# Other row and part orders for the spectrum and z transfers of an FFT convolution followed by a soft mixture of experts

## The chip, the cores and the metric

The kernel runs on one core of one Trainium2 chip. The metric is device time in microseconds of one execution, lower is better. The time before is 910.25 us, the median of 3 runs (909.78 to 915.08). All data are 4-byte floats.

## The reference

A long convolution of 8 sequences (5696 positions, 128 channels) with one filter through the FFT, and behind it a soft mixture of experts with 32 slots over all 45568 positions:

```python
Xf = np.fft.rfft(x, n=L, axis=1)              # x: (8, 5696, 128), L = 2*5696
Hf = np.fft.rfft(h, n=L, axis=0)
y = np.fft.irfft(Xf * Hf[None], n=L, axis=1)[:, :S, :]
x = y.reshape(B * S, D)
logits = x @ phi                              # (45568, 32)
d = softmax(logits, axis=0)                   # over the positions
slot_input = (d.T @ x).reshape(8, 4, 128)
slot_out[e] = np.maximum(slot_input[e] @ w1[e], 0) @ w2[e]
c = softmax(logits, axis=1)                   # over the slots
return c @ slot_out
```

## The kernel before

The transform is done as matrix products in two steps, with N1 = 90 and N2 = 64. A position is n1 * 64 + n2, and a frequency has a first index k (90 values) and a second one. The 64 values of n2 are used in two halves of 32: HALF = 32, and the columns n2 and 63 - n2 are added and subtracted beforehand, on GpSimd (`fold`, L217). A chunk is CH = 4 columns n2 of one half; a group is one sequence, or the filter (group 0), and has NJ = 8 chunks, so there are 9 x 8 = 72 chunks.

**Stage A** (`stage_a`) transforms one chunk along n1. For the frequencies below LOW (here 60) it makes 2 x 2 matmuls with 64 columns of the table s1 into two PSUM banks; ScalarE copies them to a tile fst of 128 rows x 4 KB (L243), in which rows 0 to 63 belong to one half and rows 64 to 127 to the other. For the frequencies from LOW on ("high") it does this once for two chunks, in four strips of 32 rows. The tile goes to the spectrum buffer f in DRAM, laid out as frequency, n2, real and imaginary, channel. One DMA is issued for each half (60 rows x 4 KB), and for a high tile one for each chunk and half (30 rows x 4 KB). The tile has 4 buffers.

**Stage B** (`load_g`, `stage_b1`, `stage_b2`) takes 8 frequencies at a time: it loads gt (128 rows: frequency parity and n2; 4 frequencies of 1 KB each), multiplies with the table wt (L284), multiplies with the filter's spectrum on VectorE (L304, L312), multiplies with the table vt (L327), and copies the result z to the tile zst (L332). In zst the rows alternate between two parts o = 0, 1. The first MAIN = 64 frequencies go to the buffer zm in DRAM (part, frequency, n2 half index r, real and imaginary, channel), one DMA for each part with every second row; the other 26 go to the buffer zr in four DMAs (or with shorter rows).

**Stage C** takes 8 values of r at a time, a "pair" T; there are 32 pairs. `load_main` loads zc from zm (128 rows: part and frequency; 8 KB each), `load_rest` loads zx from zr. `stage_c1` multiplies with the tables im and ir (L412, L417), and the rest of stage C does the soft mixture's logits and sums. There is one zc buffer in the main loop; after it, a second one called zd is added.

The order is written out by hand. A step t of the main loop does stage A of chunk t, stage B of up to two units of an earlier group (`slot_b`, LAG_B = 9 steps behind), and in every second step stage C1 of the pair T = (t - 27)/2. Stage A's and B's stores are put into a list `pending`, and `flush()` issues them (all carry the line L225). Nearly all DMAs are issued by SP's queue, in order: a DMA whose buffer or data isn't ready holds up those behind it. The issues there: x loads (L198), f, zm and zr stores (L225), gt loads (L270, three ahead), zc loads (L374, issued after the C1 of the pair before), zx loads (L385).

After the loop come the last pairs, the experts' products, and the output: 24 stores of 768 or 1024 KB (L897) and one last store of 256 KB (L901), which writes the last 64 positions of all 8 sequences:

```python
out=ov[:, NV * RW * N2:, :].rearrange("b (j n) d -> b j (n d)", n=CH),
in_=o_[:, n, :, :].rearrange("p q d -> p (q d)"))
```

Its DRAM side is 8 batches x 16 rows x 2 KB, its SBUF side 128 rows x 2 KB.

Of the kernel before, what the change touches and what calls it, by code (L numbers as in the profile page):

```python
# [11 lines left out]
F32 = mybir.dt.float32  # L12
# [6 lines left out]
def transform_tables(S, N1, N2, CH, LOW, MAIN, XR):  # L19

    N, R1, HALF, P = N1 * N2, S // N2, N2 // 2, 2 * N2
    k1 = np.arange(N1)  # L30
    alpha = np.pi * (k1 + 0.5) / N1
    m1 = np.arange(R1) - (N1 - 1) / 2
    a1 = np.outer(m1, alpha)
    part = np.stack([np.cos(a1), -np.sin(a1), -np.cos(a1)], 1)
    s1 = np.zeros((P, 2, 3, N2 + HALF))
    for i, r in enumerate((slice(0, R1), slice(XR - R1, XR))):
        s1[r, i, :, 0:LOW] = part[:, :, 0:LOW]
        s1[r, i, :, N2:N2 + N1 - LOW] = part[:, :, LOW:]
    a0 = np.outer(alpha, np.arange(N1 // 2) + 0.5)
    part = np.stack([np.cos(a0), -np.sin(a0), -np.cos(a0)], 1)  # L40
    NP = N1 // 2
    im = np.zeros((2, MAIN, 2, N2))
    ir = np.zeros((2, 2, HALF, N2))
    for o in range(2):
        for c in range(2):
            im[o, :, c, 0:NP] = part[0:MAIN, o + c]
            ir[o, c, 0:N1 - MAIN, 0:NP] = part[MAIN:, o + c]
    k2 = np.arange(N2)
    omega = np.pi * (k1[:, None] + 2 * N1 * k2[None] + 0.5) / N
    m2 = np.arange(HALF) - (N2 - 1) / 2  # L50
    a2 = m2[None, :, None] * omega[:, None, :]
    w = np.concatenate([np.cos(a2), np.sin(a2)], 1)
    back = np.arange(N2).reshape(2, HALF).T.reshape(-1)
    NU = (NP + 1) // 2
    turn = (N1 - 1) / 2 * alpha[:, None] + (N2 - 1) / 2 * omega
    wq = np.zeros((2, N2, NP, N2))
    vq = np.zeros((2, N2, NU, 2, N2))
    tn = np.zeros((2, N2, 2, (NU + 1) // 2, 2, 2))
    for a in range(2):
        wq[a] = w[a::2].transpose(1, 0, 2)  # L60
        for q in range(NP):
            vq[q % 2, :, q // 2, a] = w[2 * q + a][back].T
            tn[q % 2, :, 0, q // 4, a, q // 2 % 2] = np.cos(turn[2 * q + a]) / N
            tn[q % 2, :, 1, q // 4, a, q // 2 % 2] = np.sin(turn[2 * q + a]) / N
    im, ir, wq, vq, tn = [t.reshape(P, *t.shape[k:]) for t, k in
                          ((im, 2), (ir, 3), (wq, 2), (vq, 2), (tn, 2))]
    return [np.ascontiguousarray(t, dtype=np.float32) for t in (s1, im, ir, wq, vq, tn)]
# [3 lines left out]
def kernel(  # L71
# [24 lines left out]
    nc = tc.nc  # L96
    P = 128
    B, S, D = x.shape
    NSL = moe_phi.shape[1]
    E, _, F = moe_w1.shape  # L100
    SPE = NSL // E
    NFC = F // P
    N1, N2 = 90, 64
    R1, HALF, NP = S // N2, N2 // 2, N1 // 2
    CH = 4
    NJ = HALF // CH
# [5 lines left out]
    HP = P // 2  # L112
    NQ = NJ // 2
    assert S == R1 * N2 and R1 == N1 - 1 and D == P and CH == Q == 4
    LOW, MAIN = 60, HP
    XR = -(-R1 // 16) * 16
    ctx.enter_context(tc.manual_schedule())

# [1 line left out]
        nc.inline_tensor(t, f"tab_{n}").ap()  # L120
        for n, t in zip(("s1", "im", "ir", "w", "v", "turn"),
                        transform_tables(S, N1, N2, CH, LOW, MAIN, XR))]
    fd = [nc.dram_tensor(f"f_{g}", (N1, N2, 2, D), F32, kind="Internal").ap() for g in range(B + 1)]
    zm = [nc.dram_tensor(f"zm_{b}", (2, MAIN, HALF, 2, D), F32, kind="Internal").ap() for b in range(B)]
    zr = [nc.dram_tensor(f"zr_{b}", (2, 2, HALF, HALF, D), F32, kind="Internal").ap() for b in range(2)]
    cd = nc.dram_tensor("c_t", (P, B * NQ, Q, 2, MH), F32, kind="Internal").ap()

# [23 lines left out]
    front = ExitStack()  # L151
# [69 lines left out]
    pending = []  # L221
# [8 lines left out]
    def stage_a(c, high):  # L230

        g, j = divmod(c, NJ)
        st = apool.tile([P, CH, 2, D], F32, name="fst", tag="fst", bufs=4)
        if high:
            groups = [(c_, o, HALF, slice(HP, HP + HALF)) for c_ in (c - 1, c) for o in range(2)]
        else:
            groups = [(c, o, HP, slice(0, HP)) for o in range(2)]
        for q in range(2):
            p = bank()
            for i, (c_, o, m, cols) in enumerate(groups):  # L240
                nc.tensor.matmul(p[i * m:(i + 1) * m, :], s1[:, g // B, q + o, cols], columns(c_, o),  # L241
                                 start=True, stop=True)
            nc.scalar.activation(st[:, :, q, :],  # L243
                                 p[:, :].rearrange("p (n d) -> p n d", d=D), AF.Copy)
        k0, k1 = (LOW, N1) if high else (0, LOW)
        for i, (c_, o, m, _) in enumerate(groups):
            n0 = o * HALF + CH * (c_ % NJ)
            pending.append(partial(
                nc.sync.dma_start,
                out=fd[g][k0:k1, n0:n0 + CH, :, :].rearrange("k n c d -> k (n c d)"),  # L250
                in_=st[i * m:i * m + k1 - k0, :, :, :].rearrange("k n c d -> k (n c d)")))
        if high:
            for c_ in (c - 1, c):
                del folded[c_]
# [61 lines left out]
    def stage_b2(u):  # L316
        g, w, us = parts(u)
        if g == 0:
            return
        m = len(us)  # L320
        y_ = prods.pop(u)
        bz = bps.tile([P, 2, 2, 2 * D], F32, name="bz", tag="bz")
        for o, (i, n) in enumerate(us):
            for q in range(n):
                r = slice(q * HP, (q + 1) * HP)
                for a in range(2):
                    nc.tensor.matmul(bz[a * HP:(a + 1) * HP, q, o, :], vt[r, i, a, :],  # L327
                                     y_[r, a * m + o, :, :].rearrange("p c d -> p (c d)"),
                                     start=True, stop=True)
        n = us[0][1]  # L330
        st = bpool.tile([P, 2, 2, 2 * D], F32, name="zst", tag="zst", bufs=3)
        nc.scalar.activation(st[:, 0:m, 0:n, :].rearrange("p o q x -> p q o x"),  # L332
                             bz[:, 0:n, 0:m, :], AF.Copy)
        k = m * n
        sv = st[:, :, :, :].rearrange("p o q x -> p (o q) x")
        for o in range(2):
            if 8 * w < MAIN:
                pending.append(partial(
                    nc.sync.dma_start,
                    out=zm[g - 1][o, 8 * w:8 * w + 2 * k].rearrange("(q a) r c d -> (a r) q (c d)", a=2),  # L340
                    in_=sv[o::2, 0:k, :]))
                continue
            k0 = 8 * w - MAIN
            for c in range(2):
                pending.append(partial(
                    nc.sync.dma_start,
                    out=zr[g % 2][o, c, k0:k0 + 2 * k].rearrange("(q a) r d -> (a r) q d", a=2),
                    in_=sv[o::2, 0:k, c * D:(c + 1) * D]))
# [17 lines left out]
    def load_main(T):  # L366
        if T >= NT:
            return
        b, j = divmod(T, NQ)
        t_ = zring.pop(0)  # L370
        zring.append(t_)
        zs[T] = t_
        n = 2 * CH
        nc.sync.dma_start(  # L374
            out=t_[0][:, :, :, :, :].rearrange("p h n c d -> p (h n c d)"),
            in_=zm[b].rearrange("o k r c d -> (o k) r (c d)")[:, j * n:(j + 1) * n].rearrange(
                "p r x -> p (r x)"))

    def load_rest(T):
        if T >= NT:  # L380
# [243 lines left out]
    for i in range(8):  # L624
        nc.scalar.dma_start(
            out=zr[i // 4][i // 2 % 2, i % 2, N1 - MAIN:].rearrange("k (j r) d -> (k j) (r d)", r=2 * CH),
            in_=zring[0][1][0:4 * (HALF - N1 + MAIN), :, :, :].rearrange("p h n d -> p (h n d)"))
# [114 lines left out]
    for q in range(Q):  # L742
        r = slice(q * NSL, (q + 1) * NSL)
        nc.gpsimd.tensor_copy(out=rep4[r, :, :],
                              in_=ident[r, r].unsqueeze(1).broadcast_to([NSL, Q, NSL]))
# [17 lines left out]
    for V in range(T, NT):  # L763
# [30 lines left out]
        else:  # L794
            for i in range(4 * (V - T - 1), min(4 * (V - T), E), 2):
                nc.sync.dma_start(
                    out=w2s[:, i:i + 2, :, :],
                    in_=moe_w2[i:i + 2].rearrange("e (p c) d -> p e c d", p=P))
# [6 lines left out]
    p = bank()  # L805
# [8 lines left out]
    p = bank()  # L814
# [5 lines left out]
                  ap=[own.ap[0], [NSL + SPE, E], [1, SPE]])  # L820
# [6 lines left out]
    for g in range(EG):  # L827
        for f0 in range(0, F, FH):
            p = bank()
# [3 lines left out]
            dst = hid[:, g, :, f0 // NFC:(f0 + FH) // NFC]  # L833
# [6 lines left out]
    for g in range(EG):  # L840
        for k0 in range(0, NFC, 4):
            p = bank()
            for k in range(4):
# [3 lines left out]
                out=hidT[:, g, k0:k0 + 4, :], in_=p[:, :].rearrange("p (k c) -> p k c", k=4))  # L847
# [9 lines left out]
    p = bank()  # L857
# [18 lines left out]
    for b in range(B):  # L876
        for w0 in range(0, NV, G4):
            n = min(G4, NV - w0)
# [10 lines left out]
            for q in range(Q):  # L889
                dst = o_[:, 0:n + lone, q, :]  # L890
# [7 lines left out]
                out=ov[b, t0:t0 + n * RW * N2, :].rearrange("(w p n) d -> p w (n d)", p=P, n=CH),  # L898
                in_=o_[:, 0:n, :, :].rearrange("p w q d -> p w (q d)"))
            if lone:  # L900
                nc.sync.dma_start(  # L901
                    out=ov[:, NV * RW * N2:, :].rearrange("b (j n) d -> b j (n d)", n=CH),
                    in_=o_[:, n, :, :].rearrange("p q d -> p (q d)"))
# [29 lines left out]
```

## Time and profile before

| | |
|---|---|
| median of 3 runs | 910.25 us |
| the profiled execution, its time | 909.23 us |
| its span, first to last instruction | 907.4 us |
| PE (TensorE matmul) busy | 760.2 us, 84% |
| PEld (weight load) busy | 387.7 us, 43% |
| DVE (VectorE) busy | 601.4 us, 66% |
| ACT (ScalarE) busy | 436.8 us, 48% |
| POOL (GpSimd) busy | 399.8 us, 44% |
| mean granted TensorE clock | 0.903 |
| DMA, all queues | 278.33 MB, 307 GB/s |
| HBM read / written | 147.94 / 129.00 MB |
| ACT waiting at L243 for an f store (free fst) | 27.6 us in 11 waits |
| PE waiting at L284 for a gt load | 33.0 us in 10 waits |
| first and last f store issued | 15.2 and 656.2 us |
| first and last zc load issued | 175.7 and 767.3 us |

The span is the profiled execution's, and the work is counted within it. The page gives the busy time of each engine, the span in 40 slices with a digit for tenths of busy time, the DMA queues, and the chain of waits that ended last, followed back from the end. The DMA share is the mean of the 16 DMA engines' busy share; overlapping packets can take it above 1. In a list of groups, `f<-fst` reads "f written from fst".

### The profile page before, as it was taken

To read this page: it belongs to the slowest core of one execution; us is meant where nothing else is said; L and a number is where in the kernel's file an instruction comes from. 1 tells how busy PE (TensorE), PEld (TensorE's weight loads), DVE (VectorE), ACT (ScalarE), POOL (GpSimd) and SP (SyncE) were. 2 spreads that over 40 slices of the span, in tenths; PEclk is the share of its full clock that TensorE was granted. 3 is DMA by queue.
4 is the path that set the end of the run, shared out by engine and by line. 5 is a ranking of instruction groups with operands and counts; after the bars stand their busy time and mean duration, and the time that the engine had idled before them with its cause. 6 is when DMAs were issued, how large, how long until landed. Compare 5 with 4: busy or idle time off the path is not lost.

```text
span 907.4 us, 21291 instructions
## 1 busy us (share of the span) xinstructions
PE 760.2 (84%) x8308; PEld 387.7 (43%) x8308; DVE 601.4 (66%) x896; ACT 436.8 (48%) x880; POOL 399.8 (44%) x353
## 2 busy tenths in 40 slices
PE   6857778689999989999998999799888877767893
PEld 2212233234444444444444444344444434344793
DVE  2029767568778867886877787678778766653552
ACT  2423234335556545665655655456544444563441
POOL 4634322444555655655655566456332224651000
PEclk9979889999999999999999999899988888766855
DMA  8989999999999999999999999999998768540798
GB/s 267 318 275 343 293 296 337 298 314 376 341 291 375 361 326 308 372 358 299 357 364 335 295 373 348 303 308 346 306 291 304 264 200 341 186 166 1 292 406 335
DMA packets 170443, 278.33 MB, mean 307 GB/s; under 512 B 13543, under 2 KB 128231, under 8 KB 165135
## 3 DMA queue, kind: packets, MB, share of 16 engines
q1 hardware_dynamic: 169336, 275.74, 89.7%
q10 hardware_dynamic: 1008, 1.25, 0.5%
q8 instruction: 66, 1.08, 0.5%
q14 instruction: 33, 0.27, 0.1%
HBM read 147.94 MB, written 129.00 MB: 305 GB/s over the span
## 4 chain that ended last, share of the span: by engine, by line
PE 47%; DMA 23%; ACT 8%; POOL 8%; DVE 6%; issue 6%; SPq 1%; ACTq 0%; DVEq 0%; POOLq 0%
PE bank L241 9%; DMA gt<-f 9%; PE bt L284 9%; PE bz L327 6%; POOL y L430 5%; PE bank L412 4%; DMA f<-fst 4%; PE op L886 3%; PE bank L439 3%; PE bank L417 3%; PE bank L448 2%; DMA zx<-zr 2%; ACT fst L243 2%; DMA out_dram<-o 2%; PE bank L527 2%
## 5 line engine op out<-in xcount | busy, mean ns | idle before, releaser
L241 PE MATMUL bank<-x,s 128*32 128x512 f32 (+1 forms) x1152 | 218.0, 620 | 12.9 <-POOL x L217 8.4
L217 POOL TENSOR_TENSOR x<-xc 128x512 f32<-128x512 f32 x144 | 180.4, 1278 | 107.2 <-PE bank L241 86.5
L284 PE MATMUL bt<-gt,wt 64*64 64x256 f32 x1620 | 125.0, 419 | 72.8 <-DMA gt<-f 33.0
L430 POOL TENSOR_TENSOR y<-y,op 128x512 f32<-128x512 f32 x64 | 77.6, 1213 | 206.8 <-DVE op L404 204.3
L304 DVE TENSOR_TENSOR pi<-bt,Hi 128x1024 f32<-128x1024 f32 x96 | 113.0, 1177 | 83.5 <-PE bt L284 83.3
L243 ACT ACTIVATE fst<-bank 128x512 f32<-128x512 f32 x216 | 122.8, 592 | 86.0 <-PE bank L241 57.7
L332 ACT ACTIVATE zst<-bz 128x1024 f32<-128x1024 f32 x96 | 93.3, 972 | 128.3 <-PE bz L327 109.4
L284 PEld LDWEIGHTS bt<-gt,wt 64*64 64x64 f32 x1620 | 58.3, 141 | 151.2 <-issue 79.1
L312 DVE TENSOR_TENSOR yf<-bt,pi 128x512 f32<-128x512 f32 x192 | 119.4, 663 | 3.3
L304 DVE TENSOR_TENSOR bt<-bt,Hr 128x1024 f32<-128x1024 f32 x96 | 113.0, 1177 | 0.0
L241 PEld LDWEIGHTS bank<-x,s 128*32 128x32 f32 (+1 forms) x1152 | 55.1, 126 | 129.8 <-issue 93.6
L327 PE MATMUL bz<-yf,vt 64*64 64x256 f32 x1440 | 110.4, 404 | 0.0
L327 PEld LDWEIGHTS bz<-yf,vt 64*64 64x64 f32 x1440 | 64.3, 143 | 25.5 <-issue 4.2
L512 POOL TENSOR_TENSOR L<-L,rs 128x512 f32<-128x512 f32 x32 | 33.5, 1048 | 91.6 <-DVE rs L511 66.4
L404 DVE TENSOR_TENSOR y<-bank,y 128x512 f32<-128x512 f32 x32 | 22.1, 692 | 76.7 <-ACT y L420 76.5
L439 PE MATMUL bank<-ident,y 109*128 109x109 f32 x512 | 62.7, 273 | 7.9 <-ACT yt L441 7.9
L504 ACT ACTIVATE L<-L 128x512 f32<-128x512 f32 x32 | 20.2, 630 | 94.7 <-POOL L L501 94.6
L430 POOL TENSOR_TENSOR y<-y,om 128x512 f32<-128x512 f32 x54 | 63.9, 1183 | 2.1
L439 PEld LDWEIGHTS bank<-ident,y 109*128 109x128 f32 x512 | 52.9, 149 | 19.4 <-POOL x L217 14.7
L412 PE MATMUL bank<-zc,im 64*64 64x512 f32 x480 | 60.8, 623 | 0.0
L441 ACT ACTIVATE yt<-bank 128x360 f32<-128x360 f32 x128 | 53.0, 482 | 7.7 <-PE bank L439 7.3
L420 ACT ACTIVATE y<-bank 128x512 f32<-128x512 f32 x32 | 19.1, 596 | 72.6 <-PE bank L417 72.6
(101 smaller groups left out, 862.5 us busy)
## 6 DMA issues: line engine op xcount, KB each, us to landing
gt<-f SPq DMA_DIRECT2D x99, 512.0 KB
f<-fst SPq DMA_DIRECT2D x144, 240.0 KB
zm<-zst SPq DMA_DIRECT2D x128, 256.0 KB
zc<-zm SPq DMA_DIRECT2D x30, 1024.0 KB
xc<-in_x_dram SPq DMA_DIRECT2D x32, 768.0 KB
f<-fst SPq DMA_DIRECT2D x144, 120.0 KB
out_dram<-o SPq DMA_DIRECT2D x16, 1024.0 KB
zx<-zr SPq DMA_DIRECT2D x30, 512.0 KB
```

Of the source, the lines that this page charges most:

```text
L217: nc.gpsimd.tensor_tensor(out=y_[:, o, :, :], in0=near, in1=far, op=AL.subtract if o else AL.add)
L241: nc.tensor.matmul(p[i * m:(i + 1) * m, :], s1[:, g // B, q + o, cols], columns(c_, o), start=True, stop=True)
L243: nc.scalar.activation(st[:, :, q, :], p[:, :].rearrange("p (n d) -> p n d", d=D), AF.Copy)
L284: nc.tensor.matmul(bt[q * HP:(q + 1) * HP, a, o, :], wt[r, 2 * i + q, :], t_[r, 2 * o + q, :, :].rearrange("p c d -> p (c d)"), start=True ...
L304: nc.vector.tensor_tensor(out=p_, in0=pv, in1=h_, op=AL.mult)
L312: nc.vector.tensor_tensor(out=y_[r, 0:k, c, :], in0=pv[:, :, c, :], in1=pi[r, 0:k, 1 - c, :], op=op_)
L327: nc.tensor.matmul(bz[a * HP:(a + 1) * HP, q, o, :], vt[r, i, a, :], y_[r, a * m + o, :, :].rearrange("p c d -> p (c d)"), start=True, sto ...
L332: nc.scalar.activation(st[:, 0:m, 0:n, :].rearrange("p o q x -> p q o x"), bz[:, 0:n, 0:m, :], AF.Copy)
L412: nc.tensor.matmul(ps[o, c][h_ * HP:(h_ + 1) * HP, :], im[r, c, :], zt[r, h_, :, c, :], start=True, stop=False)
L430: eng.tensor_tensor(out=part_, in0=part(v, 0), in1=o_[:, :, :], op=sign)
L439: nc.tensor.transpose(p[:, i * TR:(i + 1) * TR], ys[T][0:TR, k * CH + i, 0:D], ident[0:TR, 0:TR])
L441: nc.scalar.activation(yt[:, k * CH:(k + 1) * CH, :, :], of_tokens(p), AF.Copy)
```

## The change

The frequencies are split at 64 in place of 60 (LOW = HP = 64). The low tile then has 64 + 64 full rows, and the high tile 4 strips of 32 rows of which 26 hold frequencies and 6 are empty (zero columns of s1). f gets 64 + 32 = 96 rows of frequencies, so that the empty ones have a place. Each fst tile is stored by one DMA of 128 rows, whose DRAM side is written out as a pattern with three dims. In f the n2 then stand in the order chunk, half, column in place of half, chunk, column, and the table wt's rows are permuted (`front`) to match.

z's rows for the first 64 frequencies come out of the product with vt by part and then r (no `back` permutation for them), and zm is laid out as frequency, part, r. A unit's z goes out in one DMA of 128 rows in place of two of 64. The zc load then reads zm through a pattern of part, frequency, row.

```diff
+    front = np.arange(N2).reshape(2, HALF // CH, CH).transpose(1, 0, 2).reshape(-1)
...
-        wq[a] = w[a::2].transpose(1, 0, 2)
+        wq[a] = w[a::2].transpose(1, 0, 2)[front]
         for q in range(NP):
-            vq[q % 2, :, q // 2, a] = w[2 * q + a][back].T
+            vq[q % 2, :, q // 2, a] = w[2 * q + a][back if 2 * q >= MAIN else slice(None)].T
...
-    LOW, MAIN = 60, HP
+    LOW, MAIN = HP, HP
...
-    fd = [nc.dram_tensor(f"f_{g}", (N1, N2, 2, D), F32, kind="Internal").ap() for g in range(B + 1)]
-    zm = [nc.dram_tensor(f"zm_{b}", (2, MAIN, HALF, 2, D), F32, kind="Internal").ap() for b in range(B)]
+    fd = [nc.dram_tensor(f"f_{g}", (LOW + HALF, N2, 2, D), F32, kind="Internal").ap() for g in range(B + 1)]
+    zm = [nc.dram_tensor(f"zm_{b}", (MAIN, 2, HALF, 2, D), F32, kind="Internal").ap() for b in range(B)]
...
-        k0, k1 = (LOW, N1) if high else (0, LOW)
-        for i, (c_, o, m, _) in enumerate(groups):
-            n0 = o * HALF + CH * (c_ % NJ)
-            pending.append(partial(
-                nc.sync.dma_start,
-                out=fd[g][k0:k1, n0:n0 + CH, :, :].rearrange("k n c d -> k (n c d)"),
-                in_=st[i * m:i * m + k1 - k0, :, :, :].rearrange("k n c d -> k (n c d)")))
+        k0, m = (LOW, HALF) if high else (0, LOW)
+        j0 = j - high
+        v = fd[g][k0, 2 * CH * j0]
+        dst = [[CH * 2 * D, P // m], [N2 * 2 * D, m], [1, CH * 2 * D]]
+        pending.append(partial(
+            nc.sync.dma_start,
+            out=bass.AP(tensor=v.tensor, offset=v.offset, ap=dst),
+            in_=st[:, :, :, :].rearrange("p n c d -> p (n c d)")))
...
+        if 8 * w < MAIN:
+            pending.append(partial(
+                nc.sync.dma_start,
+                out=zm[g - 1][8 * w:8 * w + 2 * k].rearrange("(q a) o r c d -> (a o r) q (c d)", a=2),
+                in_=sv[:, 0:k, :]))
+            return
         for o in range(2):
-            if 8 * w < MAIN:
-                pending.append(partial(
-                    nc.sync.dma_start,
-                    out=zm[g - 1][o, 8 * w:8 * w + 2 * k].rearrange("(q a) r c d -> (a r) q (c d)", a=2),
-                    in_=sv[o::2, 0:k, :]))
-                continue
...
-            in_=zm[b].rearrange("o k r c d -> (o k) r (c d)")[:, j * n:(j + 1) * n].rearrange(
-                "p r x -> p (r x)"))
+            in_=zm[b].rearrange("k o r c d -> o k r (c d)")[:, :, j * n:(j + 1) * n].rearrange(
+                "o k r x -> o k (r x)"))
```

## The prediction

> **What bounds the kernel now.** I read the page first, then the list of DMA issues, then engine and DMA load by stage, and last the end of the span in quarter microseconds, because the one old transfer that has the new ones' form is the last one issued. The page:
>
> ```profile
> PE   6857778689999989999998999799888877767893
> DMA  8989999999999999999999999999998768540798
> GB/s 267 318 275 343 293 296 337 298 314 376 341 291 375 361 326 308 372 358 299 357 364 335 295 373 348 303 308 346 306 291 304 264 200 341 186 166 1 292 406 335
> ...
> q1 hardware_dynamic: 169336, 275.74, 89.7%
> ...
> PE 47%; DMA 23%; ACT 8%; POOL 8%; DVE 6%; issue 6%; SPq 1%; ACTq 0%; DVEq 0%; POOLq 0%
> ```
>
> TensorE and the DMA engines are both nearly full up to slice 30 (680 us). The chain of waits has PE in front, DMA behind it, and the queue of SP, from which nearly all DMAs are issued, at 1%. So bytes count here, and the number of issues hardly does. The issues that the change touches, and the one that it should be compared with (the last line here):
>
> ```profile
> f<-fst SPq DMA_DIRECT2D x144, 240.0 KB
> zm<-zst SPq DMA_DIRECT2D x128, 256.0 KB
> zc<-zm SPq DMA_DIRECT2D x30, 1024.0 KB
> ...
> f<-fst SPq DMA_DIRECT2D x144, 120.0 KB
> ...
> zd<-zm SPq DMA_DIRECT2D x2, 1024.0 KB
> ...
> out_dram<-o SPq DMA_DIRECT2D x1, 256.0 KB
> ```
>
> The load by stage (columns: stretch; its length; busy time of PE, PEld, DVE, ACT, POOL with instructions; granted clock; mean busy share of 16 DMA engines; GB/s):
>
> ```profile
> 400.00:500.00 100.00, 93.21 (x1068) 45.17 (x1064) 75.66 (x119) 55.76 (x113) 56.62 (x49) 0.98 1.01 340
> 800.00:844.00 44.00, 30.25 (x373) 20.11 (x374) 14.83 (x38) 18.70 (x54) 11.74 (x15) 0.69 0.19 70
> 898.00:899.00 1.00, 0.00 (x0) 0.00 (x0) 0.00 (x0) 0.00 (x0) 0.00 (x0) 0.50 1.05 410
> ```
>
> One engine's pace follows: 340/16 = 21 GB/s in the mixed traffic of the loop, 410/16 = 25.6 GB/s in the plain stores at the end. Now the very end:
>
> ```profile
> 903.00:903.25 0.25, 0.00 (x0) 0.00 (x0) 0.00 (x0) 0.00 (x0) 0.00 (x0) 0.50 0.86 336
> 903.50:903.75 0.25, 0.00 (x0) 0.00 (x0) 0.00 (x0) 0.00 (x0) 0.00 (x0) 0.50 0.28 107
> 904.75:905.00 0.25, 0.00 (x0) 0.00 (x0) 0.00 (x0) 0.00 (x0) 0.00 (x0) 0.50 0.06 25
> 905.00:905.25 0.25, 0.00 (x0) 0.00 (x0) 0.00 (x0) 0.00 (x0) 0.00 (x0) 0.50 0.06 25
> 905.25:905.50 0.25, 0.00 (x0) 0.00 (x0) 0.00 (x0) 0.00 (x0) 0.00 (x0) 0.50 0.06 25
> 905.50:905.75 0.25, 0.00 (x0) 0.00 (x0) 0.00 (x0) 0.00 (x0) 0.00 (x0) 0.50 0.06 25
> 905.75:906.00 0.25, 0.00 (x0) 0.00 (x0) 0.00 (x0) 0.00 (x0) 0.00 (x0) 0.50 0.02 8
> ```
>
> A share of 0.06 is one engine of 16. Alone it still moves 25 GB/s and no more, for 1 us and a bit: 4 x 0.25 x 25 + 0.25 x 8 = 27 KB. The last transfer issued is L901's 256 KB (at 895.5 us). Its DRAM side counts 8 batches outside and 16 rows inside; its SBUF side counts 128 partitions. Over 16 engines each would hold 16 KB of it, over 8 engines 32 KB. A last engine with at least 27 KB left fits 8, the outer count of the DRAM side, and 16 only if that engine had lagged by chance.
>
> **Edits that cost nothing.** TensorE, ScalarE, VectorE and GpSimd keep every instruction and every size: the low matmuls had 64 columns already, the tables only change their order, the loads of gt stay 128 rows of the same lengths. SP issues less: 288 f stores become 72 + 36 = 108, and 128 zm stores become 64. At their median issue times, 0.407 us for f and 0.609 for zm, that is (288 - 108) x 0.407 + 64 x 0.609 = 112 us less on SP; if the new f form costs zm's 0.609 us, 90 us. It lies beside other work, as SP holds 1% of the chain (9 us), and no cover is needed for a saving. Padding adds bytes: f was 144 x 240 + 144 x 120 KB = 53.08 MB and becomes 108 x 512 KB = 56.62 MB. The zm stores keep their bytes and still count 128 rows on both sides (part, half and row merge into one step of 256 elements), so they stay spread.
>
> **The form of the f stores and zc loads.** The DRAM side of a low f store now counts 2 (halves of n2) x 64 rows x 1024 elements, of a high one 4 x 32 x 1024, and of a zc load 2 x 64 x 2048: each outer count is small, as in L901, and the SBUF side has 128 rows. How many engines carry them no old row shows directly. The two ends are 16 engines (nothing lost) and as many as the outer count: 2, 4 and 2. I take the outer count, because L901 is the nearest row and its end fits 8. The bytes of the busiest engine then are:
> - low f: 72 x 512 KB = 37.75 MB on 2 engines: 18.87 MB each
> - high f: 36 x 512 KB = 18.87 MB on 4: 4.72 MB each
> - zc and zd: 32 x 1024 KB = 33.55 MB on 2: 16.78 MB each
> - all the rest, (278.33 - 53.08 - 33.55) / 16 = 191.70 / 16 = 11.98 MB
>
> That is 40.37 + 11.98 = 52.35 MB if the same engines serve all three, against 278.33/16 = 17.4 MB before. The long rows at 25.6 GB/s take 1577 us, the rest at the loop's 21 GB/s 570 us: 2147 us. Beside it stand the stretches without traffic for these engines: 800 to 844 us, where the feed-forward part runs at a share of 0.19 (44 x 0.81 = 36 us), and some 15 us until the first f store is issued (15.2 us). Sum 2198, and 909.23 - 907.4 = 1.8 us around the span: 2200 us. The profiled 909.23 lies 1.0 us under the median of 910.25, so no correction.
>
> **Who waits.** A low store takes 262 KB / 25.6 = 10 us on its two engines, a zc load 20 us; before, a chunk had (656.2 - 15.2)/71 = 9.0 us. A chunk now brings 10 + 2.6 (half of a high store) + 10 (half of a zc load) us, and with the other transfers' share about 30 us. As every other transfer has a part on the two engines, gt, x and zx loads land behind that backlog too. ACT then waits for a free fst (4 buffers, L243), PE for gt (L284) and zc (L412). SP, which issues in order, stands at the next zc load (one buffer, until PE is through L412), with the zx load and the high store behind it. I count no bubble for this, as SP has by then issued the low store of the same chunk, 10 us of work, against the 1.9 us that a pair's L412 matmuls take in the chain of waits. If that cover fails at every one of 32 pairs, 32 x 10 = 320 us come on top. PE itself would not be late even at the clock of 0.50 that the end shows: 760 x 0.903/0.5 = 1373 us.
>
> [...]
>
> **Rivals.**
> - *Spread after all (not slower).* If the 128 SBUF rows set the split, each engine carries 56.62/16 = 3.54 MB of f, as 15 engines did with 53.08/15 = 3.54, and the zc loads are as before. What is left is SP's relief, at most its 9 us of the chain: 900 to 911 us, say 903. For it: the 27 KB could be a lag. It decides as soon as a zc load lands in the 3 us that 1 MB takes at 340 GB/s.
> - *Confined, but not all on the same engines.* Were the engines of the three forms all different, the busiest would hold 18.87 + 11.98 MB: 737 + 570 + 53 = 1360 us. Were only stores held to the outer count, as L901 is a store: 23.59 MB / 25.6 + (191.70 + 33.55)/16 MB / 21 = 921 + 670, with the same 53 us: 1645 us. Were only the loads: 655 + 739 + 53 = 1447 us.
> - *Confined, and bubbles besides.* 2200 + 320 = 2520 us, if SP's stop at the zc load drains the two engines each time.
>
> **How the numbers follow.** Confined with most of the bubbles covered has 0.82, confined with them 0.05, partly 0.04, spread 0.09. The point is 2200. Its own bounds: 52.35 MB all at 25.6 GB/s, 2045 + 53 = 2098; all at 21, 2493 + 53 = 2546. I lean to the lower end, since 77% of the bytes are rows of 4 and 8 KB. With the quiet stretches possibly filled (53 us less) the range goes down to 2040, and with half of the bubbles and a mixed pace up to 2450. About 1% is what a measurement can tell from no change: spread splits into 0.04 faster and 0.05 within, and the rest is slower, 0.91.
>
> **What would show it.** Right: mean DMA share below 0.45 although the chain is mostly DMA; about 282 MB at some 128 GB/s; PE under 40% busy; waits of ACT for f<-fst and of PE for zc and gt that grow to hundreds of us; stretches in the loop at 50 to 60 GB/s (two engines alone); no more than a small change after 800 us of the old span. Wrong: a DMA share still near 1.0 at 300 GB/s, which is the spread rival, or zc loads that land in a few us while f stores queue (or the reverse), which is the rival of partly confined forms.

## The result and the profile after

The changed kernel takes 2142.07 us (median of 4 runs, 2139.89 to 2142.77), the kernel before 910.01 us in the same comparison: 2.351 times as long, with a 95% interval of 2.342 to 2.360. The span of the profiled execution is 2138.1 us.

The page of the changed kernel, with the lines that answer to those shown of before:

```profile
PE   4324254443325433344444332543334434653377
...
DMA  5233344433333333343343333333334334553439
...
q1 hardware_dynamic: 164696, 279.25, 39.5%
...
DMA 65%; PE 16%; SPq 10%; POOL 3%; ACT 2%; issue 2%; DVE 1%; another core or an unknown queue 0%; DVEq 0%; ACTq 0%; POOLq 0%
...
f<-fst SPq DMA_DIRECT2D x108, 512.0 KB
...
zm<-zst SPq DMA_DIRECT2D x64, 512.0 KB
zc<-zm SPq DMA_DIRECT2D x30, 1024.0 KB
```

The main DMA queue kept the 16 engines busy for 89.7% of the span before. Now it is 39.5%, and yet the chain of waits is 65% DMA: the work waits for a few of them. How many is read from short stretches. The busy time by stretch (columns as in the prediction; DMA share and GB/s are the last two), first in the tail, where a load of 1 MB of zc's form (into zd, the second buffer) runs by itself, then in the main loop:

```profile
1950.00:1955.00 5.00, 0.60 (x4) 0.36 (x4) 4.26 (x5) 0.60 (x1) 3.24 (x3) 0.57 0.13 50
1955.00:1960.00 5.00, 0.00 (x0) 0.00 (x0) 1.11 (x3) 0.63 (x1) 1.53 (x2) 0.50 0.13 54
1960.00:1965.00 5.00, 0.00 (x0) 0.00 (x0) 0.00 (x0) 0.00 (x0) 0.00 (x0) 0.50 0.13 52
```
```profile
1005.00:1010.00 5.00, 0.00 (x0) 0.00 (x0) 0.00 (x0) 0.00 (x0) 0.00 (x0) 0.50 0.13 52
1010.00:1015.00 5.00, 0.00 (x0) 0.00 (x0) 0.00 (x0) 0.00 (x0) 0.00 (x0) 0.50 0.39 144
1015.00:1020.00 5.00, 0.00 (x0) 0.00 (x0) 0.00 (x0) 0.00 (x0) 0.00 (x0) 0.50 0.13 52
```

A share of 0.13 is 2 engines of 16 (0.125), and 52 GB/s is 26 GB/s for each. In four of these six stretches no engine of the core computes at all.

That f stores and zc loads sit on the same two is read from a zc load that follows an f store. The f store is issued at 985.33 us, the zc load at 987.42 us. From 993 to 995 us the DMA share is 0.13, with packets of the store's 4 KB alone and 14 engines idle; the load's 8 KB packets start at 999 us only. Had the load two other engines, it could have started there. The chain of waits shows this load (start, us, what), against the 20 us that one takes by itself:

```profile
987.42 35.33 DMA zc<-zm
```

The waits name the transfers (engine, line and what was waited for: us in total, times, longest):

```profile
PE bank L414 <- DMA zc<-zm: 597.4, 30, 24.5
...
PE bt L286 <- DMA gt<-f: 430.8, 38, 41.1
...
ACT fst L244 <- DMA f<-fst: 86.4, 10, 15.5
```

PE waited 33.0 us at the gt loads before and 430.8 us now, although those loads themselves were not changed: a part of each stands on the two engines behind other transfers (e1 and e2 show which).

### The profile page after: what moved, and what is told of

The parts are those of the page before. It is cut to its first block, busy times and chain, and to the rows that moved or that the text cites. A ratio compares the mean times of both kernels' runs of the same rounds, so it can differ in the third digit from the quotient of the medians.

```text
span 2138.1 us, 20952 instructions
## 1 busy us (share of the span) xinstructions
PE 910.5 (43%) x8308; PEld 440.0 (21%) x8308; DVE 601.4 (28%) x896; ACT 441.4 (21%) x880; POOL 398.5 (19%) x353
## 2 busy tenths in 40 slices
DMA packets 165800, 281.83 MB, mean 132 GB/s; under 512 B 8039, under 2 KB 122727, under 8 KB 160495
## 3 DMA queue, kind: packets, MB, share of 16 engines
q1 hardware_dynamic: 164696, 279.25, 39.5%
## 4 chain that ended last, share of the span: by engine, by line
DMA 65%; PE 16%; SPq 10%; POOL 3%; ACT 2%; issue 2%; DVE 1%; another core or an unknown queue 0%; DVEq 0%; ACTq 0%; POOLq 0%
DMA zc<-zm 28%; DMA gt<-f 17%; DMA f<-fst 7%; SPq L226 7%; DMA zx<-zr 4%; DMA zr<-zst 4%; DMA zd<-zm 3%; PE bank L242 3%; PE bank L414 3%; PE bt L286 3%; POOL y L432 2%; SPq L272 2%; PE op L888 1%; PE bz L329 1%; PE bank L419 1%
## 5 line engine op out<-in xcount | busy, mean ns | idle before, releaser
L414 PE MATMUL bank<-zc,im 64*64 64x512 f32 x480 | 111.9, 1041 | 598.5 <-DMA zc<-zm 597.4
L286 PE MATMUL bt<-gt,wt 64*64 64x256 f32 x1620 | 159.5, 517 | 450.3 <-DMA gt<-f 430.8
L242 PE MATMUL bank<-x,s 128*32 128x512 f32 (+1 forms) x1152 | 237.3, 677 | 63.8 <-ACT fst L244 55.5
L286 PEld LDWEIGHTS bt<-gt,wt 64*64 64x64 f32 x1620 | 72.3, 174 | 549.4 <-issue 487.2
L414 PEld LDWEIGHTS bank<-zc,im 64*64 64x64 f32 x480 | 34.9, 214 | 653.7 <-issue 632.7
L329 PE MATMUL bz<-yf,vt 64*64 64x256 f32 x1440 | 132.4, 469 | 0.0
L329 PEld LDWEIGHTS bz<-yf,vt 64*64 64x64 f32 x1440 | 76.8, 170 | 36.3 <-issue 16.2
L306 DVE TENSOR_TENSOR pi<-bt,turn 128x1024 f32<-128x1024 f32 (+1 forms) x12 | 14.1, 1176 | 199.3 <-PE bt L286 199.3
L419 PE MATMUL bank<-zx,ir 26*64 26x512 f32 x480 | 46.9, 850 | 36.7 <-DMA zx<-zr 36.7
```

Source lines behind the costliest of these rows:

```text
L286: nc.tensor.matmul(bt[q * HP:(q + 1) * HP, a, o, :], wt[r, 2 * i + q, :], t_[r, 2 * o + q, :, :].rearrange("p c d -> p (c d)"), start=True ...
L306: nc.vector.tensor_tensor(out=p_, in0=pv, in1=h_, op=AL.mult)
L414: nc.tensor.matmul(ps[o, c][h_ * HP:(h_ + 1) * HP, :], im[r, c, :], zt[r, h_, :, c, :], start=True, stop=False)
L419: nc.tensor.matmul(p[h_ * HP:(h_ + 1) * HP, :], ir[r, :], zx[r, h_, :, :], start=False, stop=True)
```

## The experiments

The theory is the prediction's: a transfer runs on as many engines as the outermost count of its DRAM side, up to 16, and always on the same ones (which they are, no view here shows). Its main rival on the chip is that the new places of the rows in DRAM are slow to write and read, whoever carries them. A weaker rival is that each of the three forms has engines of its own.

**e1, the f stores cut by part.** The same bytes to the same addresses, but 64 or 32 rows outside:

```diff
-        dst = [[CH * 2 * D, P // m], [N2 * 2 * D, m], [1, CH * 2 * D]]
...
+        for i in range(P // m):
+            n0 = 2 * CH * j0 + CH * i
...
+                out=fd[g][k0:k0 + m, n0:n0 + CH, :, :].rearrange("k n c d -> k (n c d)"),
+                in_=st[i * m:(i + 1) * m, :, :, :].rearrange("k n c d -> k (n c d)")))
```

> The changed kernel with its f stores cut into one DMA per part (64 or 32 rows), same addresses, same bytes; the zc load stays as changed (2 x 64 rows). Theory (a transfer runs on as many engines as the outer count of its DRAM side, and always the same first ones): only zc is confined, 16.78 MB on 2 engines on top of 15.5 MB spread; the first 175 us as before, then about 27.8 MB at 25.1 GB/s, then 107 us of tail: about 1390 us. Rival (the new order of rows in DRAM is slow to write and read): addresses are unchanged, so about 2140. Rival (each form has engines of its own, the busiest decides): near 1390 too, but then e2 alone must reach 2140.

Measured: 1432.61 us. The addresses are those of the changed kernel, so for f their order is not what costs most of the time. PE's wait for gt is down to 46.9 us.

**e2, the zc load cut by part.**

```diff
+        for o in range(2):
+            nc.sync.dma_start(
+                out=t_[0][o * HP:(o + 1) * HP, :, :, :, :].rearrange("p h n c d -> p (h n c d)"),
+                in_=zm[b].rearrange("k o r c d -> o k r (c d)")[o, :, j * n:(j + 1) * n].rearrange(
+                    "k r x -> k (r x)"))
```

> The changed kernel with its zc load cut into two DMAs of 64 rows, one per part; f stores stay as changed (2 x 64 and 4 x 32 rows). Theory: only f is confined, 23.59 MB on the first 2 engines on top of 14.1 MB spread, over the front alone: 15 + 33.7 MB at 25.1 GB/s + 251 us behind the last f store = about 1600 us. Rival (row order in DRAM): about 2140. Rival (own engines for each form): about 2140 if f alone decided.

Measured: 1615.82 us. PE's wait for zc falls from 597.4 to 90.8 us, while the wait for gt stays what it was in the changed kernel: with e1, it is the f stores that gt loads stand behind. Its row in the groups of instructions (the last part is PE's idle time before it and what ended most of that):

```profile
L286 PE MATMUL bt<-gt,wt 64*64 64x256 f32 x1620 | 158.2, 514 | 453.8 <-DMA gt<-f 432.5
```

**e3, both cuts.**

> Both cuts at once: same DRAM layouts, padding, tables and the single zm store of the change, but every f store and zc load has 64 or 32 rows outside. Theory: all on 16 engines, 895 to 915 us; against the kernel before, 15 engines with 53.08 MB of f become 16 with 56.62 MB, and 64 zm issues are saved, so -1% to +1%. Additive engines (the same two serve all): e1 - e3 and e2 - e3 add up to 2142 - e3 = about 1240 us, as 490 + 700. Rival (row order in DRAM): about 2140.

Measured: 957.93 us, 1.052 times the kernel before (1.048 to 1.057). Some 96% of the loss is gone: (2142 - 958) / (2142 - 910). The parts nearly add up: e1 - e3 = 474.7, e2 - e3 = 657.9, together 1132.6 us, against 2142.1 - 957.9 = 1184.2. Had each form its own engines, one would expect about the longer of e1 and e2, 1616 us; the sum fits the zc load above, which waits for the f store's two engines. But 958 is not the 895 to 915 that the theory gave. It calls for a second cause, which e5 to e11 look for.

**e4, a gap in zm.** The kernel before, in which one unused frequency between the two parts keeps the zc load's 128 rows from merging into equal steps:

```diff
-    zm = [nc.dram_tensor(f"zm_{b}", (2, MAIN, HALF, 2, D), F32, kind="Internal").ap() for b in range(B)]
+    zm = [nc.dram_tensor(f"zm_{b}", (2, MAIN + 1, HALF, 2, D), F32, kind="Internal").ap() for b in range(B)]
...
+            in_=bass.AP(tensor=zm[b].tensor, offset=zm[b][0, 0, j * n].offset,
+                        ap=[[(MAIN + 1) * HALF * 2 * D, 2], [HALF * 2 * D, MAIN], [1, n * 2 * D]]))
```

> The kernel before with nothing of the change, but one unused frequency (32 KB) between the two parts of zm, so that the zc load's DRAM side no longer merges into 128 equal steps and counts 2 x 64. Same bytes, same row lengths, same issues. Theory: zc on 2 engines, 16.78 MB on top of 15.3 MB spread: about 1380 us, near e1. Rival (row order or pitch in DRAM): rows lie as before but for a gap, so 910 us.

Measured: 1423.4 us. A gap of 32 KB costs 511 us, and PE's idle time in front of the zc matmuls, which was 0.0 us before, becomes 378.0 us (the group's row of before, then of e4):

```profile
L412 PE MATMUL bank<-zc,im 64*64 64x512 f32 x480 | 60.8, 623 | 0.0
L412 PE MATMUL bank<-zc,im 64*64 64x512 f32 x480 | 113.6, 1054 | 378.0 <-DMA zc<-zm 377.1
```

**e7, only the high tiles as changed.** The f part of the change with old z, low tiles cut by 64, high tiles in one store with 4 x 32 rows:

```diff
+        if not high:
+            for i in range(P // m):
...
+        else:
+            v = fd[g][k0, 2 * CH * j0]
+            dst = [[CH * 2 * D, P // m], [N2 * 2 * D, m], [1, CH * 2 * D]]
```

> As e6, but the high tile is stored by the change's one DMA, 4 x 32 rows outside; low tiles in two DMAs of 64. Theory (engines = outer count): 18.87 MB on 4 engines, 4.72 MB each in place of 1.18, so 3.54 MB more on each of these; at 25.1 GB/s 141 us more work for them, of which the front's slack (e6 moves 17.6 MB an engine = 702 us in 910) takes some: 940 to 1050 us. Were an outer count of 4 spread over 16 as well: as e6.

Measured: 1032.98 us, 104 us above e6 (the next but one), its like without this store. Behind the high store issued at 716.30 us the DMA share from 721.5 to 723 us is 0.26 at 101 GB/s: four engines at 25 GB/s each. Their 3.54 MB more each cost less than the 141 us that were worked out; presumably part of it falls into time in which they had been free.

**e5, the zc load of the kernel before in two halves.** Old places in DRAM, two DMAs of 64 rows in place of one of 128:

```diff
+        for o in range(2):
+            nc.sync.dma_start(
+                out=t_[0][o * HP:(o + 1) * HP, :, :, :, :].rearrange("p h n c d -> p (h n c d)"),
+                in_=zm[b][o].rearrange("k r c d -> k r (c d)")[:, j * n:(j + 1) * n].rearrange(
+                    "k r x -> k (r x)"))
```

> The kernel before with one edit: its zc load cut into two DMAs of 64 rows (rows 0 to 63, then 64 to 127), addresses in DRAM as before, both with 64 rows outside. It asks why e3, with all 16 engines everywhere, is 47 us above the kernel before. Theory P (a load into one half of the partitions is written at half the pace): zc rows of 8 KB slow down as in e3, the whole 945 to 955 us. Rival R (z's rows lie 64 KB apart in the new zm, 32 KB in the old, and the memory is slow at that): 910 us. Rival S (the single zm store or the f padding costs it): 910 us.

Measured: 959.19 us, 1.047 (1.041 to 1.053). This one cut costs as much as e3's whole rest over the kernel before (45 us).

**e6, the change's f part alone, cut.** e3's f with zm, its stores and the zc load as before.

> The change's f part alone, cut by 64 or 32 rows (LOW = 64, padded high rows, new order of n2), with zm's layout, stores and the zc load as before. Theory: 16 engines with 56.62 MB in place of 15 with 53.08 MB, the same per engine, 905 to 915 us. Rival S (the padding or the order of f costs e3's 47 us): 930 to 955 us. If the free 16th engine had been worth something: 890 to 903 us.

Measured: 928.6 us, 1.014 (1.009 to 1.019): neither the 905 to 915 of the theory nor the whole of e3's rest. The 15 engines that the expectation gives the stores of before fit a stretch of the kernel before (23 to 27 us) in which almost only f's 4 KB packets move: a DMA share of 0.93, with 15/16 = 0.94. The theory by itself would give 60 or 30 rows 16; why it is less, no run shows. On how many engines e6's stores ran was not measured by itself. The 46 us of e5 and the 15 us of e6 together exceed the 45 us of e3; why they don't add up was not isolated.

**e8, the change's z part alone, cut.** f as before.

> The change's z part alone: zm by frequency, part, r, one store of 128 rows a unit, zc loaded by two DMAs of 64 rows; f as before. Theory P: about as e5 (945 to 955 us) and as e3, since the zm store of 128 rows costs nothing. Rival R (64 KB between z's rows): 945 to 960 us while e5 stays at 910. Rival S with the single store as the cost: the same, but with zc rows of 8 KB as fast as before.

Measured: 952.63 us, 1.042 (1.037 to 1.047), not to be told from e5. With the old rows (e5) and the new (e8) alike, the 64 KB between z's rows and the single zm store are not what costs the 5%.

**e9, two DMAs again, but each of every second row.** As e5, with `t_[0][e::2]` and every second row of zm in place of a half:

```diff
+        for e in range(2):
+            nc.sync.dma_start(
+                out=t_[0][e::2, :, :, :, :].rearrange("p h n c d -> p (h n c d)"),
+                in_=zm[b].rearrange("o k r c d -> (o k) r (c d)")[e::2, j * n:(j + 1) * n].rearrange(
+                    "p r x -> p (r x)"))
```

> The kernel before with its zc load cut into two DMAs of 64 rows as in e5, but each takes every second row of the 128 (partitions 0, 2, 4 and 1, 3, 5) in place of one half. Theory P (it is the half of the partitions that slows e5's loads): 905 to 920 us, 8 KB rows as fast as before. Rival (two smaller DMAs, or 64 rows as such): 950 to 960 us as e5.

Measured: 916.81 us, 1.003 (1.000 to 1.007). Two DMAs of 64 rows cost next to nothing; two DMAs that each fill one half of the partitions cost 46 us. One load of 1 MB in the tail, by stretches of 1 us (e5 first, the load into zd; then e9, the last zc load, with the zx load behind it from the third line on):

```profile
819.00:820.00 1.00, 1.00 (x15) 0.69 (x8) 0.00 (x0) 0.24 (x1) 0.72 (x1) 1.00 0.90 184
820.00:821.00 1.00, 1.00 (x15) 0.86 (x16) 0.58 (x1) 1.00 (x3) 0.00 (x0) 1.00 1.07 243
821.00:822.00 1.00, 1.00 (x34) 0.80 (x33) 0.71 (x4) 1.00 (x4) 0.25 (x1) 1.00 1.04 213
```
```profile
780.00:781.00 1.00, 1.00 (x13) 0.95 (x11) 0.45 (x1) 1.00 (x3) 0.00 (x0) 1.00 0.76 287
781.00:782.00 1.00, 1.00 (x34) 0.82 (x32) 0.71 (x4) 1.00 (x4) 0.12 (x1) 1.00 0.96 401
782.00:783.00 1.00, 1.00 (x18) 0.55 (x10) 0.97 (x2) 1.00 (x5) 0.93 (x1) 1.00 0.91 324
```

Divided by the busy share, e5 moves 204 to 227 GB/s and e9 356 to 418. Over the whole run, the median 8 KB packet takes 309 ns in the kernel before and in e9, and 567 ns in e5. Slow rows in DRAM are not the reason: e8's two loads read the same addresses of zm as e9's (64 KB from row to row, the second DMA 32 KB behind the first) but fill one half of the partitions each; its median is 562 ns, and it takes 952.63 us against e9's 916.81. A busy share near 1 did not mean full pace here: 1.04 went with 213 GB/s in e5, 0.96 with 401 in e9. The pair e5 and e9 fits theory P; what slows the loads that fill one half, no run shows.

**e10, the split at 64 without padding.** The kernel before with `LOW, MAIN = HP, HP`: low stores of 64 rows, high ones of 26, no more bytes than before.

> [...] Theory (e6's +1.4% is its 1.3% more bytes): 908 to 920 us. Rival (the 64-row form or the split at 64 costs it): as e6, 925 to 932 us.

Measured: 922.03 us, 1.011 (1.007 to 1.014), between the two. The split at 64 costs about 1% without any padding, so the padding and the new order of n2 are at most the rest of e6's 1.4% (the intervals overlap). The edit makes two changes at once, low stores of 64 in place of 60 rows and high ones of 26 in place of 30; which of them costs this was not isolated.

**e11, 16 x 8 rows.** As e4, but with an unused frequency behind every 8:

```diff
+    zm = [nc.dram_tensor(f"zm_{b}", (2, MAIN // 8, 9, HALF, 2, D), F32, kind="Internal").ap() for b in range(B)]
...
+                        ap=[[9 * HALF * 2 * D, 16], [HALF * 2 * D, 8], [1, n * 2 * D]]))
```

> The kernel before with an unused frequency behind every 8 in zm, so that the zc load's DRAM side counts 16 x 8 rows in place of one run of 128: a pattern of three dims like the change's and e4's, but 16 outside. Theory (engines = outer count, up to 16): 16 engines, 905 to 925 us. Rival (any such three-dim pattern, or gaps, are carried by few engines): as e4, about 1420 us.

Measured: 955.55 us, 1.047 (1.042 to 1.052). It is far from e4's 1423 us, so neither a gap nor a third dim by itself confines a transfer to a few engines; in the forms run here (2, 4 and 16 outside) the outer count does. But it misses the 905 to 925, and its last zc load is as slow as e5's load above:

```profile
817.00:818.00 1.00, 1.00 (x32) 0.80 (x22) 0.75 (x3) 1.00 (x4) 0.55 (x1) 1.00 1.04 201
818.00:819.00 1.00, 1.00 (x11) 0.33 (x9) 0.97 (x3) 1.00 (x6) 0.50 (x1) 1.00 0.99 180
819.00:820.00 1.00, 1.00 (x13) 0.36 (x12) 0.97 (x2) 0.60 (x4) 0.38 (x1) 1.00 0.98 193
```

All engines are busy at about half the pace here as well (182 to 197 GB/s for the busy share, a median of 559 ns for 8 KB packets), though all 128 partitions are in one transfer. So a load can be as slow without being kept to one half of the partitions. The reason stays open: no run shows which engine takes which row.

No version that was run is faster than the kernel before.

## Why the prediction was right

**The outer count.** The choice that carried the forecast was to read L901's end as 8 engines, and to take the outer count for the new forms. The count is right: the stretches at 0.13 and 52 GB/s show 2 engines, e7 shows 4 for an outer count of 4, e4 shows the confinement with nothing of the change in the kernel, and e11 shows that 16 outside lifts it. The row that it was read from was thin: it shows one engine alone for some 1 us, which a lag gives too, and no run shows on how many engines L901 ran. That part of the reading was lucky.

**The sum.** 52.35 MB on the busiest engine was right as a term: bytes were 281.83 MB in all (282 forecast). That the same engines serve all three forms was assumed, as no row of before shows it; e1 and e2 add up as the same two engines would (1132.6 of 1184.2 us). 2200 was 58 us too high. The pace of the long rows measured 26 GB/s (52 GB/s over two), which makes their 40.37 MB 1553 us in place of 1577. The remainder, 2138 - 1553 - 53 = 532 us for 11.98 MB, is 22.5 GB/s in place of 21, if the quiet 53 us are right; it was not measured by itself. By this account the pace of the short transfers was mis-sized by 38 us, and that of the long rows by 24.

**The waits.** A zc load was to take 20 us: in the tail the one into zd runs from 1946 to about 1966 us. A chunk with zc loads was to take about 30 us: from the first zc load at 412.1 us (chunk 25) to the last f store at 1758.7 it is 1346.6 / 46 = 29.3 us. Counting the bubbles at nothing was right: between 100 and 1700 us the trace has under 2 us in all in which fewer than two DMA engines are busy. The wait for a free fst was expected to grow to hundreds of us; it is 86.4, so that sign was wrong. Presumably PE, held up by gt and zc, filled the buffers less often. PE was to be busy for under 40% and is for 43%: its granted clock fell from 0.903 to 0.682, and the same matmuls took 910.5 us in place of 760.2.

**The rivals.** "Confined in part" is what e1, e2 and e4 are, each by an edit: 1447 us was worked out for loads alone (1432.6 and 1423.4 measured) and 1645 for stores alone (1615.8). "Spread after all", at 903 us, stays untried in its own form, one transfer of 128 rows on 16 engines: neither f's places nor the new zm's allow equal steps there. Its nearest kernel, e3, takes 958 us, but its loads fill half of the partitions each, at little more than half the pace, which e5 prices at 46 us. What the rival's own form would take is not shown.

## What to carry to other kernels

Before merging transfers, write down the pattern that each side carries after merging, and look at the outermost count on the DRAM side: a "transfer of 128 rows" whose DRAM side is 2 x 64 ran on 2 engines here, and a single unused row that broke the merging cost 511 us. Keep the long dim outside (a layout whose 128 rows have one step), or issue one transfer for each outer step; and if that splits a load into SBUF, try pieces that take every second partition and not one half (917 against 959 us, tried in the kernel before). An outer count of 16 brought all engines back, but not their full pace (e11, 956 us). When DMA is on the chain of waits but its mean share is low, look at stretches of a few us: here a share that sat at 0.13, 2 of 16, named the cause.

## What was not expected of the hardware

An issue on SP's queue itself took long, up to 20.45 us, while the transfers ahead of it ran on few engines. SP's zx and zy issues in the tail of the changed kernel, behind the zd and zc loads (columns: start, us, queue and line, transfer):

```profile
1919.80 4.01 SPq L376 DMA_DIRECT2D zc<-zm  x1
1923.85 17.13 SPq L387 DMA_DIRECT2D zx<-zr  x1
...
1946.01 4.42 SPq L376 DMA_DIRECT2D zd<-zm  x1
1950.54 17.13 SPq L387 DMA_DIRECT2D zy<-zr  x1
```

The zx issue had a median of 0.35 us before; now it is 8.31 us. These two stand for 17.13 us, about as long as the load ahead of them still runs on its two engines, and everything behind them on SP stands as well. The stores stand too: the 20.45 us are an f store's issue. SP comes to 10% of the chain of waits, 7 of them at the stores (L226), with 64 + 180 fewer DMAs to issue.
